# Each engine's instruction list written into the program's main part instead of into a block with one part per engine

## The chip, the cores and the metric

The kernel runs on one core of a Trainium2 chip. A core has five engines that run their own instruction lists side by side: TensorE (PE, matmuls and weight loads), VectorE (DVE), ScalarE (ACT), GpSimd (POOL) and SyncE (SP, which here only issues DMAs and waits for them). They are ordered among each other by semaphores alone. The metric is the time of one execution on the device, in microseconds, and lower is better. Several executions are timed without a profiler and their median is given; one more is profiled, and it has a time of its own.

## The reference

A block of linear attention and a gated feed-forward part share one normalised input; the output is x + attention * silu(feed-forward).

```python
S, D, F = 2048, 448, 1792             # 16 heads of 28
xn = layernorm(x)                     # (1, 2048, 448) bfloat16
q, k, v = split_heads(xn @ wqkv)
pq, pk = phi(q), phi(k)               # phi(t) = where(t > 0, t + 1, exp(t)) + 1e-6
kv = einsum("bhsd,bhse->bhde", pk, v)
z = sum of pk over the tokens
num = einsum("bhqd,bhde->bhqe", pq, kv)
den = einsum("bhqd,bhd->bhq", pq, z) + 1e-6
s = merge_heads(num / den) @ wo
h = relu(xn @ w1 + b1) ** 2           # 1792 columns
g = silu(h @ w2 + b2)
return x + s * g
```

## The kernel before, in words

The 2048 tokens are cut into 16 tiles of 128 and four groups of 512. Everything stays in on-chip memory between the stages: x is loaded, normalised on VectorE and transposed; TensorE then runs the projections for k and q, the 1792-column hidden layer (L785) and its way back to 448 columns (L1091), sums over the tokens for the attention (L886), folds of the value and output weights, and a last stage in which the attention output of a tile (L1183) and its gate meet. The last two tiles, 14 and 15, have their gates computed at the very end (`gate_last`, L1138, matmuls on L1148), tile 15 in two pieces of 256 and 192 columns; each piece runs through silu, a multiplication, an addition (L1172) and a DMA to the output.

No loop runs on the chip. The Python code describes every operation by `Program.add` (L54): its engine, what it reads and writes, an estimated duration. `Program.schedule` (`one_pass`, L98) plays these through and writes out one ordered list per engine, `self.order["pe"]`, `["act"]`, `["dve"]`, `["pool"]` and `["sp"]`. DMAs are operations of the engine that issues them, SP for most, ACT for some; all of them have the helper's line L434.

`Program.emit` (L248) then turns the lists into instructions. First it hands out semaphores: one per engine that counts the engine's finished operations, one per DMA or group of DMAs. Then it works out, in the order of the planned start times, which waits every operation still needs. Up to here nothing has been emitted. L291 opens a block. `body_of(e)` (L293) makes a function that walks through the list of engine `e`: for every operation its waits (L297), then the operation itself with its semaphore increment. For SP it adds, behind the last operation, one wait for each of the 17 DMAs that write the output (L302). L306 to L310 hand these functions to the block, which opens a part of its own for each engine: GpSimd, SyncE, ScalarE, TensorE, VectorE.

Two things aren't visible as lines of `emit`. When the program is constructed (L1385), four constants are set by GpSimd and an opening barrier over all five engines is written into the main part. And the block is entered on the ExitStack of the kernel function, so it is left when the `with` on L316 ends: there each engine gets a branch to a common end, and behind it a closing barrier, in which every engine drains (DRAIN) and reports, GpSimd collects the reports, and all are released. These instructions are booked on L316. The opening barrier stands on L1385.

Of the kernel before, what the change touches and what calls it, by code (L numbers as in the profile page):

```python
# [32 lines left out]
class Op:  # L33
    def __init__(self, eng, emit, reads, writes, dur, alts, nbytes, mode, label):
        self.eng, self.emit, self.dur, self.alts, self.nbytes = eng, emit, dur, alts, nbytes
        self.reads, self.writes, self.mode, self.label = list(reads), list(writes), mode, label
        self.raw, self.deps, self.succ = set(), set(), []
        self.start = self.end = None
        self.seq = None
        self.late = 1e9  # L40
        self.prio = None
        self.sync = None
        self.group = None
        self.lead = 0.0


class Program:
# [6 lines left out]
    def add(self, eng, emit, reads=(), writes=(), dur=0.2, alts=(), nbytes=0, mode=None, label="", slow=1.0):  # L54
        op = Op(eng, emit, reads, writes, dur, alts, nbytes, mode, label)
        op.slow, op.behind, op.at = slow, None, None
        for t in op.reads:
            op.raw.add(self.writer[t])
            self.readers.setdefault(t, []).append(op)
        for t in op.writes:  # L60
            w = self.writer.get(t)
            if w is not None and w is not op:
                op.deps.add(w)
            for r in self.readers.get(t, ()):
                if r is not op:
                    op.deps.add(r)
            self.writer[t] = op
            self.readers[t] = [r for r in self.readers.get(t, ()) if r is op]
        op.raw.discard(op)
        op.deps |= op.raw  # L70
        for d in op.deps:
            d.succ.append(op)
        self.ops.append(op)
        return op
# [173 lines left out]
    def emit(self, nc, es):  # L248
        sems = {e: es.enter_context(nc.semaphore("q_" + e)) for e in self.ENGINES}
        n_dma = 0  # L250
        groups = {}
        for e in self.ENGINES:
            k = 0
            for op in self.order[e]:
                if op.group is not None:
                    if op.group not in groups:
                        groups[op.group] = es.enter_context(nc.semaphore(f"d{n_dma}")), ("d", n_dma)
                        n_dma += 1
                    op.sem, op.key = groups[op.group]
                    op.seq = 16 * sum(o.group == op.group for o in self.ops)  # L260
                elif op.nbytes:
                    op.sem, op.seq, op.key = es.enter_context(nc.semaphore(f"d{n_dma}")), 16, ("d", n_dma)
                    n_dma += 1
                elif op.label.startswith("table"):
                    op.sem, op.seq, op.key = es.enter_context(nc.semaphore(op.label)), 1, op.label
                else:
                    k += 1
                    op.sem, op.seq, op.key = sems[e], k, e
        done = {}
        waits = {}  # L270
        prev = {}
        for op in sorted(self.ops, key=lambda o: (o.start, 0 if o.eng == "pe" else 1)):
            e = op.eng
            known = dict(prev.get(e, {}))
            need = []
            deps = set(op.deps) | set(self.bankdeps.get(op, ()))
            deps.discard(op)
            for d in sorted(deps, key=lambda d: -d.end):
                if d.key == e == "pe" and d is not op.sync:
                    continue  # L280
                if known.get(d.key, 0) >= d.seq:
                    continue
                need.append((d.sem, d.seq))
                for kk, vv in done[d].items():
                    if known.get(kk, 0) < vv:
                        known[kk] = vv
                known[d.key] = max(known.get(d.key, 0), d.seq)
            waits[op] = need
            prev[e] = known
            done[op] = known  # L290
        block = es.enter_context(nc.Block())  # L291

        def body_of(e):  # L293
            def body(h):
                for op in self.order[e]:
                    for s, v in waits[op]:
                        h.wait_ge(s, v)  # L297
                    op.emit(h, e).then_inc(op.sem, 16 if op.nbytes else 1)
                if e == "sp":
                    for o in self.ops:  # L300
                        if o.nbytes and o.writes and o.writes[0][0] == "out":
                            h.wait_ge(o.sem, 16)  # L302

            return body

        block.gpsimd(body_of("pool"))  # L306
        block.sync(body_of("sp"))
        block.scalar(body_of("act"))
        block.tensor(body_of("pe"))
        block.vector(body_of("dve"))  # L310


def bass_recurrent_scan__linear_attn_block__dense_activation_squared_relu__prompt_kernel(
# [1086 lines left out]
```

## Time and profile before

| what | value |
|---|---|
| time, median of 3 runs | 144.64 us (144.61 to 145.0) |
| time of the profiled execution | 144.69 us |
| its span, first to last instruction | 143.0 us |
| mean granted TensorE clock | 0.997 |
| data moved by DMA | 12.91 MB, mean 90 GB/s |
| largest share of the chain that ended last | PE 89% |
| DMAs that write the output | 13 + 1 on SP's queue, 2 + 1 on ACT's |

The span counts only the program's own instructions; the time of an execution also holds what happens around them. The busy shares say how much of the span an engine computed: an instruction that only waits, branches or issues a DMA isn't counted as busy. In the chain of work that ended last, each row was released by the one above it. A row of a source line gives the engine, the operation, the number of its instructions, the least, median and greatest duration in nanoseconds, and the start of the first and the last in microseconds; a `q` behind an engine's name means that the engine's instruction queue handled it alone.

The first loads look like this in the timeline (start, duration, engine, line, operation, and in brackets the idle time before and what ended it):

```profile
0.80 1.28 ACT L474 ACT_TABLE_LOAD   x1 [0.80 <-PEq L1385]
0.80 0.20 POOL L376 MEMSET ident<- 128x128 bf16 x1 [0.29 <-POOLq L1385]
0.81 0.39 SPq L434 DMA_DIRECT2D x_tok<-in_A_x_dram  x1
0.84 0.58 ACTq L434 DMA_DIRECT2D w_k<-in_A_wqkv_dram  x1
0.89 0.11 DVE L375 MEMSET dum<- 128x64 uint32 x1 [0.89 <-PEq L1385]
```

SP's queue, the engine and line that waited, what it waited for, and the total in us, the number of times and the longest, over the last five microseconds:

```profile
SPq L434 <- DVE gbuf L1172: 2.3, 2, 1.6
SPq L302 <- DMA out_dram<-gbuf: 0.7, 2, 0.4
SPq L434 <- DVE gbuf L1190: 0.4, 1, 0.4
SPq L316 <- PEq L316: 0.2, 1, 0.2
```

### The profile page before, as it was taken

The numbers are of one execution on the slowest core, as the hardware profiler recorded it, in microseconds if no ns is written. First come the engines' busy times: TensorE is split into PE (matmuls) and PEld (weight loads), VectorE is DVE, ScalarE is ACT, GpSimd is POOL, SyncE is SP. The second block draws the span as 40 slices with busy tenths as digits, with TensorE's granted clock in tenths as the row PEclk, the third lists the DMA queues.
The fourth block names the chain that finished last, engine by engine and source line by source line (L and its number), as shares of the span: only waits on it lengthen the run. The fifth ranks groups of instructions, "written<-read, shape, count | busy, mean of one in ns | idle before, by whom it ended". The sixth has DMA issues, their size and how long they took to land.

```text
span 143.0 us, 3246 instructions
## 1 busy us (share of the span) xinstructions
PE 138.3 (97%) x1300; PEld 70.9 (50%) x1300; DVE 103.0 (72%) x222; ACT 78.9 (55%) x146; POOL 6.2 (4%) x40
## 2 busy tenths in 40 slices
PE   7899999999999999999999999999999999999991
PEld 7753445454444444444544444445546455555471
DVE  2845999789689897789777799785036507865874
ACT  3676997140889627697862767696139430202311
POOL 7900000000000000000000000000000000000000
PEclk9999999999999999999999999999999999999998
DMA  4999983238953100232000000000696001223032
GB/s 100 316 308 302 339 264 68 42 46 222 247 62 50 19 0 0 46 54 43 9 5 0 0 0 5 0 0 18 172 201 150 0 0 39 94 64 101 32 125 68
DMA packets 23500, 12.91 MB, mean 90 GB/s; under 512 B 14274, under 2 KB 22718, under 8 KB 23486
## 3 DMA queue, kind: packets, MB, share of 16 engines
q1 hardware_dynamic: 21470, 11.17, 30.7%
q10 hardware_dynamic: 2016, 1.54, 4.8%
q8 instruction: 10, 0.16, 0.5%
q14 instruction: 4, 0.03, 0.1%
HBM read 9.23 MB, written 1.90 MB: 78 GB/s over the span
## 4 chain that ended last, share of the span: by engine, by line
PE 89%; DMA 4%; SPq 3%; DVE 1%; issue 0%
PE pb L785 28%; PE pb L1091 22%; PE pb L1183 7%; PE pb L886 7%; PE pb L728 6%; PE pb L738 6%; DMA w<-in_B_w_dram 4%; PE pb L1108 4%; SPq L434 3%; PE pb L1148 3%; PE pb L865 1%; DVE gbuf L1172 1%; PE pb L892 1%; PE pb L1035 1%; PE pb L960 1%; PE pb L1061 1%
## 5 line engine op out<-in xcount | busy, mean ns | idle before, releaser
L785 PE MATMUL pb<-xT,w 64*128 64x512 bf16 x378 | 43.8, 376 | 0.2 <-DMA w<-in_B_w_dram 0.2
L1091 PE MATMUL pb<-w,r 64*128 64x448 bf16 x336 | 34.6, 349 | 0.0
L763 ACT ACTIVATE r<-pb,b1f 128x512 bf16<-128x512 f32 x40 | 25.7, 686 | 13.9 <-PE pb L785 13.6
L785 PEld LDWEIGHTS pb<-xT,w 64*128 64x128 bf16 x378 | 18.2, 94 | 22.3 <-DMA w<-in_B_w_dram 0.7
L1091 PEld LDWEIGHTS pb<-w,r 64*128 64x128 bf16 x336 | 16.3, 94 | 15.9 <-issue 0.4
L775 ACT ACTIVATE r<-r 128x1024 bf16<-128x1024 bf16 x15 | 15.7, 1062 | 0.3
L760 DVE TENSOR_SCALAR r<-pb,b1f 128x512 bf16<-128x512 f32 x16 | 11.7, 745 | 3.7 <-PE pb L785 3.7
L1203 DVE TENSOR_TENSOR gbuf<-pb,gbuf 128x448 bf16<-128x448 f32 x14 | 8.1, 618 | 6.6 <-PE pb L1183 6.6
L495 DVE BATCH_NORM_STATS2 st<-x_tok 128x6 f32<-128x448 bf16 x16 | 9.5, 612 | 3.6 <-DMA x_tok<-in_A_x_dram 3.6
L728 PE MATMUL pb<-w_k,xT 64*128 64x448 bf16 x98 | 11.6, 349 | 0.0
L738 PE MATMUL pb<-xT,w_q 64*128 64x512 bf16 x84 | 11.0, 376 | 0.0
L1131 ACT ACTIVATE gbuf<-gbuf 128x448 bf16<-128x448 bf16 x14 | 7.0, 570 | 6.6 <-DVE gbuf L1081 5.9
L1183 PE MATMUL pb<-w_k,pqT 64*128 64x448 bf16 x96 | 10.5, 349 | 0.0
L1081 DVE TENSOR_TENSOR gbuf<-pb,b2b 128x448 bf16<-128x448 f32 x14 | 8.0, 614 | 3.4 <-PE pb L1091 2.0
L718 DVE SCALAR_TENSOR_TENSOR pk<-pb,pk 128x448 bf16<-128x448 f32 x16 | 9.5, 617 | 0.2
L706 ACT ACTIVATE pk<-pb 128x448 bf16<-128x448 f32 x16 | 7.8, 543 | 3.4 <-PE pb L728 2.5
L886 PE MATMUL pb<-pk,xn 128*128 128x448 bf16 x48 | 9.6, 353 | 0.0
L999 DVE TENSOR_TENSOR pqT<-pqT,xT 128x2048 bf16<-128x2048 bf16 x3 | 3.7, 1222 | 8.1 <-DMA xT<-scr 8.1
L706 ACT ACTIVATE pqT<-pb 128x512 bf16<-128x512 f32 x12 | 6.5, 597 | 4.7 <-PE pb L738 4.7
L774 DVE TENSOR_TENSOR r<-r 128x1024 bf16<-128x1024 bf16 x13 | 8.5, 681 | 0.1
L922 DVE TENSOR_TENSOR zacc<-zacc,pk 128x448 f32<-128x448 f32 x13 | 8.0, 617 | 0.1
L525 DVE TENSOR_SCALAR xn<-x_tok,mv,rstd 128x448 bf16<-128x448 bf16 x16 | 7.4, 499 | 0.7 <-ACT rstd L507 0.6
(98 smaller groups left out, 133.2 us busy)
## 6 DMA issues: line engine op xcount, KB each, us to landing
w<-in_B_w_dram SPq DMA_DIRECT2D x1, 1568.0 KB, 10.8
out_dram<-gbuf SPq DMA_DIRECT2D x13, 112.0 KB, 1.7
x_tok<-in_A_x_dram SPq DMA_DIRECT2D x3, 448.0 KB, 6.7
xT<-gbuf SPq DMA_DIRECT2D x32, 32.0 KB, 2.0
w<-in_B_w_dram SPq DMA_DIRECT2D x2, 384.0 KB, 6.3
xT<-scr SPq DMA_DIRECT2D x6, 112.0 KB
w<-in_B_w_dram SPq DMA_DIRECT2D x1, 576.0 KB, 6.4
xT<-scr ACTq DMA_DIRECT2D x5, 112.0 KB
```

The costliest lines, as they stand in the source:

```text
L495: add("dve", lambda e, _: e.bn_stats(st6[:, si, :], x_tok[:, si, :]), [("x", si)], [("st", si)], 0.61, label=f"bn{si}").prio = hp(si, 0)
L706: "act", lambda e, _: e.activation(out=slot, in_=ps(buf)[0:rows, 0:n], func=AF.Exp), [buf, "actw"],
L718: lambda e, _: e.scalar_tensor_tensor(out=slot, in0=ps(buf)[0:rows, 0:n], scalar=1.0 + 1e-6, in1=slot, op0=ALU.add, op1=ALU.max),
L728: return e.matmul(ps(b)[:, 0:D], x_tile(rows, si, c), w_k[rows, c, :], start=start, stop=stop)
L738: return e.matmul(ps(b)[:, 0:512], w_q[rows, c, m * P : (m + 1) * P], x_group(rows, g, c), start=start, stop=stop,)
L760: return e.tensor_scalar(out=slot, in0=ps(b)[:, 0:512], scalar1=b1f[:, fi : fi + 1], scalar2=0.0, op0=ALU.add, op1=ALU.max)
L763: return e.activation(out=slot, in_=ps(b)[:, 0:512], func=AF.Relu, bias=b1f[:, fi : fi + 1])
L775: return e.activation(out=both, in_=both, func=AF.Square)
L785: return e.matmul(ps(b)[:, 0:512], w_1[rows, c, fi * P : (fi + 1) * P], x_group(rows, g, c), start=start, stop=stop,)
L886: last = e.matmul(ps(b)[:, 0:D], xn_cols(si, c * P, (c + 1) * P), pk[:, si, :], start=(si == 0), stop=(si == NT - 1),)
L1091: return e.matmul(ps(b)[:, 0:D], r_cols(rows, fi, si), w_2[rows, fi, :], start=start, stop=stop)
L1183: return e.matmul(ps(b)[:, 0:D], w, msb[rows, c, :], start=start, stop=stop)
```

## The change

The block is no longer opened. Each function that `body_of` makes is called at once with the engine's own handle, in the order SyncE, ScalarE, TensorE, VectorE, GpSimd, so that the instructions go into the part that is current, the main part that already holds the opening barrier. With the block go the parts per engine, the branches and the closing barrier at its end. The lists, their waits, the semaphores and SP's waits for the outputs are the same.

```diff
@@ -288,8 +288,6 @@
             waits[op] = need
             prev[e] = known
             done[op] = known
-        block = es.enter_context(nc.Block())
-
         def body_of(e):
             def body(h):
                 for op in self.order[e]:
@@ -303,11 +301,8 @@
 
             return body
 
-        block.gpsimd(body_of("pool"))
-        block.sync(body_of("sp"))
-        block.scalar(body_of("act"))
-        block.tensor(body_of("pe"))
-        block.vector(body_of("dve"))
+        for e, h in (("sp", nc.sync), ("act", nc.scalar), ("pe", nc.tensor), ("dve", nc.vector), ("pool", nc.gpsimd)):
+            body_of(e)(h)
```

## The prediction

> **What bounds the kernel now.** I read the busy shares first, then the chain that ended last near its end, then the rows of the source lines that the change touches, and then the queues of kind "instruction". The page's head:
>
> ```profile
> span 143.0 us, 3246 instructions
> PE 138.3 (97%) x1300; PEld 70.9 (50%) x1300; DVE 103.0 (72%) x222; ACT 78.9 (55%) x146; POOL 6.2 (4%) x40
> ```
>
> TensorE is busy 138.3 of 143.0 us, and the change edits none of its matmuls. So only the two ends of the span can move: about 12 us of loading in front, and the tail behind the last matmul. The chain in order of time, from 134 us on:
>
> ```profile
> 134.49 4.30 PE pb L1148 x28
> 138.78 0.02 issue
> 138.81 0.42 DVE gbuf L1161
> ...
> 140.70 0.26 DVE gbuf L1172
> ```
>
> The last computing instruction ends at 140.70 + 0.26 = 140.96 us. The 2.0 us from there to the end of the span hold the last output transfer, SyncE's waits for all the outputs (L302), and the instructions booked on L316, the line whose with-statement leaves the block. Their rows (engine, operation, count: duration in ns, first and last start in us):
>
> ```profile
> L302 SPq EVENT_SEMAPHORE  x8: 28/28/28, 141.4 to 142.5; - x8
> ```
>
> ```profile
> L316 POOLq EVENT_SEMAPHORE  x2: 17/17/17, 142.8 to 142.9; - x2
> L316 POOLq DRAIN  x1: 361/361/361, 21.9 to 21.9; - x1
> L316 PEldq DRAIN  x1: 1755/1755/1755, 138.3 to 138.3; - x1
> L316 DVEq DRAIN  x1: 297/297/297, 140.7 to 140.7; - x1
> L316 ACTq DRAIN  x1: 152/152/152, 140.9 to 140.9; - x1
> L316 SPq COMPARE_BRANCH  x1: 38/38/38, 142.6 to 142.6; - x1
> L316 SPq DRAIN  x1: 7/7/7, 142.7 to 142.7; - x1
> L316 SPq EVENT_SEMAPHORE  x1: 17/17/17, 142.9 to 142.9; - x1
> ...
> L316 PEldq EVENT_SEMAPHORE  x1: 51/51/51, 142.9 to 142.9; - x1
> ```
>
> The reader is to see that four engines stand drained early (POOL from 22.3 us on, PE from 140.1, ACT and DVE from about 141.0) and that SP alone is late: it waits for the outputs and then passes the news on to GpSimd, which releases all five. To the nanosecond the trace has SP's last wait of L302 ending at 142.529, its branch at 142.569 to 142.607, its DRAIN at 142.742, GpSimd's two semaphore steps at 142.774 and 142.853, and the release arriving on SP, ACT, DVE and PE at 142.894, 142.899, 142.905 and 142.906. TensorE's release takes 51 ns, and the span ends with it at 142.957. The time around the span is 144.69 - 142.957 = 1.73 us in the profiled execution, and no row says how it is split between front and back. That execution is 0.05 us above the median of the three runs, 144.64.
>
> **The change, part by part.** *Way into the block.* Removed in the source, but the rows show no branch there. On L1385 (the opening barrier, which stays) SP's semaphore wait ends at 0.742 and its first DMA starts at 0.810, a gap of 0.068; between that DMA's end (1.195) and the next one (1.254) it is 0.059. The difference, 0.01 us, is nothing I can price; ACT's gap is 0.054, and POOL's and DVE's (about 0.10 and 0.13) lie under the wait for x and the weights. TensorE's chain starts behind a DMA that lands at 12.0. Taken: 0, bounds 0 to 0.01.
>
> *Order of emission* (SP, ACT, PE, DVE, POOL in place of POOL, SP, ACT, PE, DVE). Each engine keeps its own list of operations and waits, the semaphores are handed out before, and no queue is moved past another. Taken: 0. What hides it is that an engine only meets its own list. If a setup instruction came or went on POOL, its price would be one MOVE, 0.04 us, under POOL's idle stretch before TensorE's first transpose at 5.2 us.
>
> *Branch out.* Only SP executes one (the single COMPARE_BRANCH), and it carries the seventeenth output's wait: eight waits of L302 take two each. That wait has to remain, as a ninth EVENT_SEMAPHORE of 28 ns at 142.569, so SP's last instruction ends at 142.597.
>
> *Closing barrier.* It goes: five DRAINs and six semaphore instructions; four of the drains lie under SP's wait. On the path lie SP's DRAIN, GpSimd's two steps and the release. With the branch, the stretch that leaves the span is 142.957 - 142.597 = 0.360 us. The new span is 142.60.
>
> *What follows the program.* The other engines then leave their lists up to 120 us earlier than now, and only SP comes late, at 142.597. Now all five come together between 142.870 (POOL) and 142.957 (PE). The trace doesn't show what is done there, so I bound it. Low: SP's closing is the longest, and what counts is SP alone, 142.911 before and 142.597 after, a gain of 0.314. High: PE's is the longest by as much as PE is behind SP in coming into the program, whose first DRAINs start at 0.000 on SP, 0.122 on DVE, 0.136 on ACT and 0.315 on PE. Then PE was last before and SP is last now, and 0.315 more goes: 0.360 + 0.315 = 0.675. Neither row is nearer, so I take the middle, (0.314 + 0.675) / 2 = 0.495 us.
>
> Sum: 144.69 - 0.495 = 144.20 for the profiled execution, and 144.64 - 0.495 = 144.15 for the median, 0.34% less. The bounds give 143.97 to 144.33.
>
> One rule bears on the branch. SP goes from the start of its branch to its DRAIN in 0.173 us, and the last packet on a queue of kind "instruction" starts at 129.7:
>
> ```profile
> q8 instruction: 10, 0.16, 0.5%
> q14 instruction: 4, 0.03, 0.1%
> ```
>
> The Trainium skill (Runtime: NRT & Kernel Launch, section "Instruction fetch mechanics") says that a taken branch whose target isn't in the loaded pages stalls the engine for a fetch; had this branch met that, the removal would be worth a packet more. The trace has no packet there, so it doesn't. The same page's "The launch sequence" lists a barrier behind every kernel, with an estimate of 1.5 us; no run here shows it, and the sum by it would still lose the 0.36.
>
> **The rivals.**
>
> *The barrier's work is done again* (no change). Whatever ends the execution must learn that all five engines are done; if that is one more collecting step that today finds all engines together, it may cost afterwards what the chain from SP's DRAIN to the release costs now, 142.957 - 142.742 = 0.215. Then only the branch goes, 0.360 - 0.215 = 0.145: 144.50. For it: the 1.73 us outside must hold such a step. Against: four engines would already be waiting in it.
>
> *Closing work is freed* (faster still). If half of the 1.73 us lies behind the program (0.87) and is split among five engines that now take turns, four of the five shares (0.69) move under SP's wait: 0.36 + 0.69 = 1.05, so 143.59. For it: POOL is idle from 22 us on. Against: engines that start together normally work side by side.
>
> *Code loading meets the last outputs* (slower). Engines that fall out of their lists early go on to other code. PE, ACT and DVE do so at 140.1 to 141.0, just when the last two outputs (issued at 140.52 and 140.99, landing 1.5 to 1.6 us later) are on the DMA engines. The two rows above give the price: 0.5% of 16 engines' 143 us is 11.4 us for ten packets, 1.14 us each. One such packet ahead of a descriptor of the last output delays its landing, and SP's last wait, by up to 1.14: 144.64 + 1.14 - 0.36 = 145.42. It decides from a delay of 0.36 on, a third of a packet. For it: the DMA engines' only late load is these outputs, so any delay is exposed. Against: today DVE's and ACT's drains at 140.7 to 140.9 show that they had their following code then, and no packet starts behind 129.7.
>
> *The change does nothing*: it would need a barrier put back at the end of the program's main part. The opening one on L1385 is there without a block, so I can't exclude it. It is counted with the first rival, as no change.
>
> **How the numbers follow.** A measurement of this kernel tells about 0.3% from no change, 0.43 us: faster is under 144.21, slower above 145.07. Chances: forecast 0.62, the barrier done again (or put back) 0.11, closing work freed 0.15, code loading 0.12. The forecast's interval of gains, 0.314 to 0.675, lies above 0.43 for (0.675 - 0.434) / 0.361 = two thirds, 0.41 of the chance; the remaining 0.21 is no change. Faster: 0.41 + 0.15 = 0.56. Same: 0.21 + 0.11 = 0.32. Slower: 0.12. The predicted time is the forecast's, 144.15; its own range is 143.97 to 144.33. The full range reaches down past the freed closing work (143.59), to 143.50, and up past the first rival (144.50) and its put-back form (144.64) by a little over the scatter, to 144.75. Outside are the code loading and a small rest below.
>
> **What would show it.** Right: no row on L316; nine waits on L302, the last ending at about 142.60 with the span; 11 instructions fewer (five DRAINs, six semaphore steps and the branch go, one wait comes), 3235; busy times of PE, DVE and ACT unchanged; a time outside the span of 1.42 to 1.78 us (the gains of 0.675 and 0.314 less the 0.360), against 1.73. A wrong step would show as follows. A rise of the time outside by about 0.2 is the barrier done again, a fall by over 0.3 the closing work freed. "Instruction" packets behind 138 us, with output landings above 1.7 us, are the code loading. A first DMA of SP away from 0.81, or a chain that reaches TensorE's stream at another time than 12.0, would make the "0" for the way in wrong, and with it the whole prediction, since every microsecond in front of 12 is on the chain.

## The result and the profile after

The changed kernel took 143.64 us in the median of four runs (143.53 to 144.04), against 144.62 us for the kernel before (144.43 to 145.0): a ratio of 0.9934 with a 95% interval of 0.9906 to 0.9962. The second comparison, with 12 runs against 35, gave 0.9952 (0.9929 to 0.9975). It is faster, and of the two sizes the smaller one is the change's own, as shown below.

The head of the page of the changed kernel:

```profile
span 142.5 us, 3235 instructions
PE 138.5 (97%) x1300; PEld 71.2 (50%) x1300; DVE 103.1 (72%) x222; ACT 79.0 (55%) x146; POOL 6.7 (5%) x40
```

The same number of computing instructions, 11 others fewer, and busy times that differ by 0.5 us at most. The lines are renumbered: before's L302, SP's waits for the outputs, is L300, and L434 is L429. No instruction is booked on the line where the with-statement ends. SP's waits are the last rows of the trace (operation, count: least, median and greatest duration in ns, first and last start in us):

```profile
L300 SPq EVENT_SEMAPHORE  x9: 17/28/28, 141.3 to 142.5; - x9
```

The least duration, 17 ns, is the point to look at. It belongs to the first of the nine (141.343 to 141.360), the only one that waits for a single semaphore. Before, the eight waits took two semaphores each, and the branch took the seventeenth: that of an early output, which had landed at 121.849. Now the pairs are shifted by one. The early output shares the ninth wait with the last output (issued at 140.959), from 142.468 to 142.496, and with it the span ends. Before, it was the eighth wait (to 142.529) that held the last output.

The outputs land as before. The rows of the DMA issues of the last five microseconds, with the least, median and greatest time from issue to landing (us) below them:

```profile
L429 SPq DMA_DIRECT2D out_dram<-gbuf x3: 332/333/333, 138.2 to 141.0; - x3
L429 ACTq DMA_DIRECT2D out_dram<-gbuf x1: 338/338/338, 140.5 to 140.5; - x1
...
DMA to landing us min/median/max: 1.5/1.6/1.7
```

The last packet on a queue of kind "instruction" starts at 129.67 us, none behind it.

What lies between the end of SP's wait for the last output and the end of the execution is the part that the change can reach, and it can be taken from every run: the stretch in the span from the profiled run, plus the time outside the span, of which each run has its own. It was 0.428 + 1.734 = 2.16 us before (mean of 97 runs of the kernel before, made beside the experiments; standard deviation 0.03), and is 0 + 1.548 = 1.55 in the 16 runs of the changed kernel. That is 0.61 us.

The spans of these runs are on record to 0.1 us, and this rounding alone gives a scatter of 0.03; in the profiled executions, whose spans are known to the nanosecond, the time outside is 1.733 before, and 1.544 and 1.541 after. The span itself scatters ten times as much: 142.72 with a standard deviation of 0.31 before, 142.31 with 0.34 after, a difference of 0.41 (standard error 0.09), which agrees with the 0.428 us of tail. So 0.61 us, 0.42%, is the change. The rest of the 0.98 us of the first comparison is scatter of the span, over only four runs; of these four only the slowest (144.04) has a trace.

### The profile page after: what moved, and what is told of

It is laid out like the page before. It is cut to its first block, busy times and chain, and to the rows that moved or that the text cites. A ratio compares the mean times of both kernels' runs of the same rounds, so it can differ in the third digit from the quotient of the medians.

```text
span 142.5 us, 3235 instructions
## 1 busy us (share of the span) xinstructions
PE 138.5 (97%) x1300; PEld 71.2 (50%) x1300; DVE 103.1 (72%) x222; ACT 79.0 (55%) x146; POOL 6.7 (5%) x40
## 3 DMA queue, kind: packets, MB, share of 16 engines
q10 hardware_dynamic: 2016, 1.54, 4.7%
## 4 chain that ended last, share of the span: by engine, by line
PE 92%; DMA 3%; DVE 2%; SPq 1%; issue 0%
PE pb L780 29%; PE pb L1086 22%; PE pb L1178 7%; PE pb L881 7%; PE pb L723 7%; PE pb L733 6%; PE pb L1103 4%; DMA w_k<-in_A_wqkv_dram 3%; PE pb L1143 3%; PE pb L860 1%; DVE gbuf L1167 1%; PE pb L887 1%; PE pb L823 1%; PE pb L795 1%; PE pb L1030 1%; SPq L429 1%
```

## The experiments

The theory: the tail behind SP's last wait leaves the span, and the time outside it shrinks because the engines have ways of different length from their last instruction to the end of the execution, of which SP's is a short one. The rivals: something in front of 12 us is faster too; or what counts outside is only how many engines come late together.

**The changed kernel and the kernel before, again.** No edit.

> The changed kernel again, to size the gain. Theory A (only the tail goes, and SP alone is late in what follows the program): the profiled pair gave 0.43 us of tail in the span, 0.03 of scatter ahead of it and 0.19 outside it, so 0.62 us without the scatter, a ratio of 0.9957. Theory B (something in front of 12 us is also faster, as the medians of the first comparison, 0.98 us apart, suggest): a ratio of about 0.993, with the first matmuls of the hidden layer starting 0.3 to 0.4 us earlier in most executions.

> The kernel before against itself, unchanged, for the scatter of the comparison and of the span. Both theories: a ratio of 1.000. If this differs from 1 by 0.2% or more, the 0.98 us of the first comparison can be scatter.

Measured: 143.83 us against 144.44 for the changed kernel, ratio 0.9952 (0.9929 to 0.9975); 144.35 for the kernel before against itself, 0.9981 (0.996 to 1.0001). Theory A's ratio was 0.9957. Unchanged code came out 0.2% fast, so a difference of 0.3 us between medians is within the scatter here, and theory B has nothing left to explain. Where the scatter sits is seen in the chains, first in that of the changed kernel (start, duration, what):

```profile
2.22 4.83 DMA w_k<-in_A_wqkv_dram
...
11.41 9.06 PE pb L780 x84
20.47 0.76 PE pb L723 x8
```

and then in that of a kernel told of below, in which TensorE gets one wait more at its very end and everything ahead of it is the same:

```profile
1.06 4.34 PE pb L1215 x39
...
10.96 9.06 PE pb L782 x84
20.03 0.76 PE pb L725 x8
```

The reader is to see the start of the long stretch of hidden-layer matmuls: 11.41 where the k weights landed at 7.05, 10.96 where they were there in time and the chain runs through TensorE's warm-up. From there on both streams have the same length, so 0.44 us of a load's landing is 0.44 us of the span. The profiled run before hung on another load, of the first hidden-layer weights (12.0), and its matmuls of L728 start at 20.50. The kernel with only the barrier put back has this point at 20.02, so it goes neither with the block nor with the barrier.

**Only the closing barrier back.**

```diff
         for e, h in (("sp", nc.sync), ("act", nc.scalar), ("pe", nc.tensor), ("dve", nc.vector), ("pool", nc.gpsimd)):
             body_of(e)(h)
+        nc.all_engine_barrier()
```

> The changed kernel with only the closing barrier put back, in the main part, without block and branch. Theory A: the barrier costs what its rows show, DRAIN to release 0.22 us in the span, and 0.19 outside it come back because all engines again come late together; so it lies 0.4 us above the changed kernel and 0.1 to 0.2 below the kernel before (ratio 0.9990). Rival (the block's parts cost something at the entry): it stays near the changed kernel, with a ratio of 0.995 or less.

Measured: 144.1 us, ratio 0.9966 (0.9944 to 0.9987), outside 1.745 us (mean of 12). The rows of the line at which the barrier is booked:

```profile
L306 POOLq EVENT_SEMAPHORE  x2: 17/17/17, 142.1 to 142.2; - x2
L306 POOLq DRAIN  x1: 714/714/714, 21.7 to 21.7; - x1
...
L306 SPq DRAIN  x1: 7/7/7, 142.1 to 142.1; - x1
L306 SPq EVENT_SEMAPHORE  x1: 17/17/17, 142.2 to 142.2; - x1
...
L306 PEldq EVENT_SEMAPHORE  x1: 51/51/51, 142.3 to 142.3; - x1
```

SP's last wait ends at 142.051 and the span at 142.303: 0.252 us, with no COMPARE_BRANCH among the rows. From the last wait to the end it is 0.252 + 1.745 = 2.00 us. The barrier is therefore worth 2.00 - 1.55 = 0.45 us, 0.25 of it in the span and 0.20 outside. The remaining 2.16 - 2.00 = 0.16 to the kernel before is the branch: from the end of SP's last wait to its DRAIN it is 0.213 us before and 0.038 here, and from that DRAIN to the end of the span 0.215 and 0.214. The expectation of 0.4 above the changed kernel held in this piece. The ratio expected with it, 0.9990, lies just outside the measured interval, in a comparison in which unchanged code came out at 0.9981; the total times alone, with intervals of 0.4%, couldn't have told the pieces apart.

**One more engine late.** These runs put one wait for the last output at the end of one or several lists; SP's own waits stay.

```diff
             body_of(e)(h)
+        last = self.order["sp"][-1]
+        nc.tensor.wait_ge(last.sem, 16)
```

> The changed kernel, where TensorE too waits for the last output at the end of its list. Nothing else is late. Theory A1 (TensorE's way out of the program is the longest, so in the changed kernel its closing work lies under SP's wait): the span grows by under 0.1 us, and the time outside the span rises from 1.54 to about 1.7. Theory A2 (the time outside shrank because fewer engines are late together, or because SP's way is shorter than that of another engine, POOL say): outside stays at 1.54 to 1.6.

Measured: outside 1.85 (mean of 12), with the span ending 0.035 us behind SP's wait: 1.89 from the wait to the end, 0.34 more than with SP alone. That is more than the 1.7 that theory A1 expected, and far above A2's 1.6. The total, 144.06 us, ratio 0.9968 (0.9945 to 0.999), agrees. TensorE's wait is a single instruction, and the time behind it isn't in the span:

```profile
L307 PEldq EVENT_SEMAPHORE  x1: 51/51/51, 142.0 to 142.0; - x1
```

With `nc.gpsimd` in the place of `nc.tensor`:

> The changed kernel, where GpSimd too waits for the last output (in place of TensorE in the run before). What is read is the time outside the span, which scatters by only 0.03 us: 1.73 with the block, 1.54 without, 1.85 where TensorE waits too. Theory A1 (each engine has a way out of the program of its own length, and TensorE's is the longest): GpSimd's is shorter than TensorE's, outside at 1.54 to 1.70. Theory A2 (it is the number of engines that are late together that counts): about 1.85, as with TensorE, since two are late here as well.

Measured: outside 2.09 (mean of 8), 2.09 from the wait to the end; the total is 144.6 us, ratio 1.0004 (0.9979 to 1.0029). One wait of 17 ns on GpSimd, which stands idle from 22 us on, takes back 0.54 of the 0.61 us that the change gained:

```profile
L307 POOLq EVENT_SEMAPHORE  x1: 17/17/17, 143.0 to 143.0; - x1
```

Theory A1's bound, that GpSimd's way is shorter than TensorE's, was wrong, and A2's 1.85 is missed as well.

With `nc.scalar`, and with `nc.vector`:

> The same with ScalarE. Theory A1: 1.54 to 1.65 outside (at the start ScalarE comes 0.14 us behind SyncE into the program, TensorE 0.32). Theory A2: about 1.85.

> The same with VectorE. Theory A1: 1.54 to 1.65 outside. Theory A2: about 1.85.

Measured: ScalarE 1.55 outside (ratio 0.9957, 0.9932 to 0.9983), VectorE 1.65 (0.9956, 0.9934 to 0.9978). Two engines late together cost nothing more if the second is ScalarE. A2 falls: with two engines late, it matters which the second is.

With all four:

```diff
+        last = self.order["sp"][-1]
+        nc.tensor.wait_ge(last.sem, 16)
+        nc.gpsimd.wait_ge(last.sem, 16)
+        nc.scalar.wait_ge(last.sem, 16)
+        nc.vector.wait_ge(last.sem, 16)
```

> The changed kernel, where all five engines wait for the last output, without a barrier. Theory A1: what counts is the longest way, TensorE's, so outside is that of the run where TensorE alone joins SyncE, 1.85. Theory A2: more than 1.85, by what each further engine adds.

Measured: outside 1.89, 0.035 behind SP's wait, 1.92 from the wait to the end (total 144.1, ratio 0.9977, 0.9958 to 0.9996). That is more than TensorE's 1.89 by little, but less than GpSimd's 2.09, although GpSimd is late here too. Theory A1 as "the longest way counts" doesn't give this.

**The last two late engines together, and another engine that waits alone.** First TensorE and GpSimd beside SP, with the first three lines of the diff above:

> The changed kernel, where TensorE and GpSimd wait for the last output beside SyncE. GpSimd beside SyncE gave 2.09 outside, TensorE beside SyncE 1.85, all five 1.89. Theory A1 alone (the longest way counts): 2.09 less the 0.04 by which TensorE's wait ends behind SyncE's, 2.05. Rival (GpSimd's way is long only while TensorE has been through before it): about 1.9, as with all five.

Measured: outside 2.05, 2.09 from the wait to the end, as expected by A1 (total 144.42, ratio 0.9995, 0.9977 to 1.0012). TensorE being late doesn't shorten the time behind GpSimd's wait; it was shorter only in the run in which ScalarE and VectorE were late as well.

Then the 17 waits on another engine than SP, which leaves SP early:

```diff
-                if e == "sp":
+                if e == "act":
```

> The changed kernel, where ScalarE instead of SyncE waits for the 17 outputs, so that SyncE too leaves early and only ScalarE is late. Theory A1 (each engine has a way out of its own, and the latest arrival sets the end): with SyncE and ScalarE late together the time outside was 1.55, as with SyncE alone at 1.54, so ScalarE's way is not longer; here 1.4 to 1.54. If it is clearly below 1.5, this version beats the changed kernel by that. Rival (SyncE's way doesn't count, the 1.54 is a fixed step behind the last engine, whichever it is): 1.54.

Measured: outside 1.46 (mean of 12), 0.09 below the changed kernel; total 143.78 us, ratio 0.9959 (0.9944 to 0.9974). The time behind ScalarE is shorter than that behind SP, and a step of 1.54 us that is the same behind every engine is out. The gain of 0.09 us is 0.06% and doesn't show in the total time, so no version is shown to beat the changed kernel.

With `"dve"` and with `"pool"`:

> The same with VectorE as the only late engine. Theory A1: 1.65 as with SyncE and VectorE late together, since VectorE was the later of the two. Rival (fixed step behind whichever is last): 1.54.

> The same with GpSimd as the only late engine. Theory A1: 2.09 as with SyncE and GpSimd late together. Rival (the 2.09 came from the two together, as 1.92 with all five late makes one think): 1.7 or less.

Measured: VectorE 1.645 outside, ratio 0.9962 (0.9942 to 0.9981); GpSimd 2.15, total 144.43, ratio 1.0001 (0.9986 to 1.0016). VectorE agrees with A1. GpSimd is 0.06 above A1's 2.09 and far from the rival's 1.7.

The traces also show part of the cause, because they go on recording semaphores behind the span. In every run one semaphore, number 2, is incremented nine times there. Where all nine come late, they are 0.02 to 0.10 us apart, except for a wait for GpSimd in some runs. How many of the nine come before the late wait ends depends on the engine: none where TensorE is late, one with ScalarE alone, two with GpSimd alone, three with VectorE alone, four with SyncE alone. So the engines take turns in the order TensorE, ScalarE, GpSimd, VectorE, SyncE; that the last four increments are made by the same engines on the way back is likely from the pattern, but not shown. The engine's own increment comes 0.11 us behind the last wait on SyncE, 0.14 on VectorE, 0.16 on ScalarE and 0.22 on TensorE, but 0.53 on GpSimd. The table has the time from the last wait (SyncE's, where it is one of the late engines) to the end of the execution, and to the ninth increment in the profiled execution:

| late engines | to the end, us | to the ninth increment, us |
|---|---|---|
| ScalarE alone | 1.46 | 0.48 |
| SyncE alone (the changed kernel) | 1.55 | 0.27 |
| SyncE, ScalarE | 1.55 | 0.43 |
| VectorE alone | 1.65 | 0.38 |
| SyncE, VectorE | 1.66 | 0.39 |
| SyncE, TensorE | 1.89 | 0.61 |
| all five, each by a wait of its own | 1.92 | 0.82 |
| all five through the barrier | 2.00 | 1.02 |
| SyncE, GpSimd | 2.09 | 0.82 |
| SyncE, TensorE, GpSimd | 2.09 | 0.82 |
| GpSimd alone | 2.15 | 0.82 |
| block: branch and barrier (the kernel before) | 2.16 | 1.20 |

Where ScalarE isn't among the late engines, the first column less the second is 1.27 to 1.28 us (1.33 with GpSimd alone): there the nine increments account for the differences between the engines. Where ScalarE is late it is less, about 1.11 with a wait of its own beside SyncE and 0.96 to 0.98 in the other three rows. Why is not shown.

## Why the prediction was right, and where its sizes were off

*What bounds the kernel, and that only the two ends can move*: right. PE's busy time is 138.3 and 138.5 us, and from the hidden layer on both chains have the same lengths.

*Way into the block, 0*: right. SP's first DMA starts at 0.810 in both traces, ACT's table load at 0.800 and 0.801, TensorE's first matmul at 1.056 in both. The chain did reach TensorE's long stretch at another time than 12.0, which the prediction had named as a sign against this step; but the kernels without the block have it anywhere from 10.89 (GpSimd alone late) to 12.02 (all five late, by waits of their own), with SP's first DMA at 0.81 in each, so this is the scatter of the loads.

*Order of emission, 0*: no sign of any effect; it wasn't tried by itself.

*Branch out and closing barrier, 0.360*: mis-sized, it is 0.428. The step that failed is "That wait has to remain, as a ninth EVENT_SEMAPHORE of 28 ns at 142.569". What the branch waited for was an output that had landed at 121.849. Its wait now shares the ninth instruction with the last output and needs none of its own behind it, so everything behind before's last wait (142.529 to 142.957) went. The experiment with the barrier alone divides it: 0.252 us barrier, 0.176 branch.

*What follows the program, 0.135 between -0.046 and 0.315*: that all five together have a longer way than SP alone was right, and the size is 0.186. The pictures behind the two bounds were not: neither SP's way nor TensorE's is the longest, but GpSimd's, of which the term has nothing. The upper bound came from the start, where TensorE is 0.315 behind SP; that TensorE's way out was measured as 0.34 longer is luck, since the traces put it down to the order of turns (0.61 against 0.27 us to the ninth increment). What changed outside is a difference of two parts. From the end of the span to the ninth increment it was 0.77 us before and is 0.27, so 0.50 less; what remains of the time outside grew from 0.96 to 1.28, for a reason that isn't shown. The middle was a guess between two bounds, and it was 0.05 low.

The sum, 0.495, thus became 0.61. The forecast's 144.15 us was 0.51 above the median that the result gives and 0.12 short of the change's own size; the other 0.39 is the scatter of the span in the first comparison, which no term of the sum held. The measured 143.64 lies below the forecast's own range, 143.97 to 144.33. It is inside the full range only because that was stretched to 143.50 for the freed closing work, so that part of the success is luck.

*The rivals.* The barrier done again: out, the time outside fell by 0.19 and the 0.215 didn't come back. Of the time behind the program the prediction says that the trace doesn't show what is done there. The traces do hold a collecting step, in both kernels: the nine increments, of which four now come before SP's last wait ends. Closing work freed: its 143.59 lies next to the measured 143.64, but for another reason. It wanted the time outside to fall by 0.69; it fell by 0.19. Its picture of engines that take turns has something to it, by the same four increments. Code loading: no packet behind 129.67 us, landings of 1.5 to 1.7 us. A barrier put back: the rows show none, and the instructions are the 3235 that were forecast.

The stall for a fetch that the Trainium skill describes for some taken branches (Runtime: NRT & Kernel Launch, "Instruction fetch mechanics") wasn't met by this branch: the last instruction packet starts at 129.7 us, 13 us ahead of it, and its 0.176 us is far from the 1.14 us that the prediction worked out for such a packet.

What stays open: why all five late together are quicker out (1.92) than GpSimd with SP (2.09). The ninth increment comes 0.82 us behind SP's wait in both, so GpSimd isn't quicker there; the difference lies in what remains, which is shorter in every run in which ScalarE is late. The ways aren't simply five constants of which the longest counts. No run here shows what ScalarE changes.

## What to carry to other kernels

Where the last instructions are waits for outputs, a closing barrier can cost twice: its own chain in the span (0.25 us here), and outside it (0.20 us), because all five engines then leave at the end and none of their turns behind the program is over by then. Let an engine with a short way out do the last wait, SyncE here, and let the others fall off their lists early; with all the waits on GpSimd alone, the piece was as long as with block and barrier (2.15 against 2.16 us). For effects of half a percent, compare the piece that the change can reach (here from the last wait to the end, at most 0.03 us of scatter) and not the total, whose loads in front scatter by 0.3.

## What the runs showed of the hardware

The way from an engine's last instruction to the end of the execution differs by engine: 1.46 us behind ScalarE, 1.55 behind SyncE, 1.65 behind VectorE, 1.85 behind TensorE when it comes 0.035 us behind SyncE, 2.15 behind GpSimd, each with a standard deviation of 0.03 to 0.04 over 7 to 16 runs, most of it rounding. These times also hold what precedes the program, which no trace here separates.

Behind the program the five engines increment one semaphore in turn, TensorE first and SyncE last of the five, before four more increments follow. The ninth comes 0.27 us behind a last wait on SyncE, 0.38 on VectorE, 0.48 on ScalarE, 0.58 on TensorE beside SyncE, and 0.82 on GpSimd, which takes 0.53 us from its wait to its own increment. With ScalarE late, what remains of the time is 0.16 to 0.31 us shorter, for a reason that these runs leave open.
